# A gated linear recurrence with a causal convolution behind it: a new order of operations and transfers, and a shorter setup

## The chip, the cores and the metric

The kernel runs on one core of a Trainium2 chip. The metric is device time in microseconds (us) from start to end of one execution. The kernel before takes 310.14 us, the median of 3 runs (310.02 to 310.45). The profile is one execution of it, with a span of 309.0 us from the first to the last instruction.

The engines are named as the profile names them: PE (TensorE, matmuls), PEld (its weight loads), DVE (VectorE), ACT (ScalarE), POOL (GpSimd), SP (SyncE, which here only issues loads). ACT also issues the stores, from its own instruction queue.

## The reference

Inputs x, r_gate and i_gate are 4 x 6336 x 256 in float32 (25,344 tokens of 256 channels in all). In short:

```python
a_base = 1 / (1 + exp(-a_param))
a_t    = exp(8 * sigmoid(r_gate) * log(clip(a_base, 1e-6, 1 - 1e-6)))
xg     = sqrt(max(1 - a_t * a_t, 1e-6)) * sigmoid(i_gate) * x
h      = a_t[:, t] * h + xg[:, t]          # along the 6336 tokens of each batch; y[:, t] = h
gate   = sigmoid(causal convolution of y over 5 tokens, per channel)
out    = (gate * (y @ w_val)) @ w_out
```

## The kernel before

The tokens are cut into 27 chunks: 512, then 23 of 1024, then 512, 512 and 256. Each chunk passes through a row of operations. A text called PLAN lists all of them, one word for each (`exp.7.0.-1` is the exp of chunk 7, half 0 of the channels; the last number is a PSUM bank), and the kernel emits them in that order. Every engine executes its own operations in the order of PLAN.

| word | engine | what it does | us of one (1024 tokens, or 512 for conv, val, out, tg, gv, xg, copies) |
|---|---|---|---|
| ldri, ldx | SP | loads r and i, and x, 1 MB each | |
| tanh | ACT | tanh of half of r and i, in one instruction | 3.6 |
| srT | PE | transposes of r | |
| exp | ACT | a_t, for half of the channels | 1.2 |
| e | POOL | a_t squared | 1.9 |
| s1, u | POOL | (1 + tanh of i), and that times x | 1.9 and 4.1 |
| xc, ux | PE, DVE | for chunks 0 and 1 alone: x copied to PSUM, then u made on DVE | |
| sq | ACT | square root for up to three chunks; the table of functions is changed before and after | |
| nT, xg, xgT | PE, DVE, PE | transpose, product, transpose back | xg 0.7 |
| scan | DVE | the recurrence | 2.3 |
| conv, tg | PE, ACT | convolution, tanh of it | tg 1.0 |
| val, gv, out | PE, DVE, PE | y @ w_val, product with the gate, product with w_out | gv 1.2 |
| osbD or osbA | DVE or ACT | copy of the result from PSUM | 1.2 or 1.0 |
| store | ACT queue | 256 KB or less to out | |

The buffers (three chunks of gates, two of x, four of u) and the loads and stores:

```python
X_PE = [0, 1]      # the chunks whose u is made through PE and DVE
NRI = 3; NX = 2; NU = 4; NOSB = 5; NTG = 2; NGV = 2

with tc.manual_schedule():
    ...
    def op_ldri(k, bank):
        c = k[0]
        n = CHUNKS[c]
        for e, src in ((0, rf), (1, if_)):
            nc.sync.dma_start(gate[:, slot(c, e), 0:n * H].rearrange("p (j d) -> p j d", d=D), toks(src, c, 0, n))

    def op_ldx(k, bank):
        c = k[0]
        nc.sync.dma_start(xr[:, c % NX, 0:CHUNKS[c] // P, :], toks(xf, c, 0, CHUNKS[c]))
    ...
    def op_store(k, bank):
        c, s = k
        o, n = subs[c][s]
        nc.scalar.dma_start(toks(of, c, o, n), osb[:, nth[k] % NOSB, 0:n // P * D].rearrange("p (q d) -> p q d", d=D))
```

Each transfer counts up a semaphore when it has landed. The program has eight of these for all loads and stores together, and hands them out in turn, in the order in which the transfers are emitted: the ninth takes the semaphore of the first, and so waits until the first has landed before it is issued. The wait stands in the queue of the engine that issues the transfer.

The setup computes the constant of each channel, and the weights are cast on ACT:

```python
nc.scalar.preload_act_table_set("natural_log_exp_and_others")
...
nc.scalar.activation(out=kex[:], in_=kps, func=ACT.Exp, scale=-1.0)
nc.vector.tensor_scalar(out=ksig[:], in0=kex[:], scalar1=1.0, scalar2=None, op0=ALU.add)
nc.vector.reciprocal(out=ksig[:], in_=ksig[:])
nc.vector.tensor_scalar(out=ksig[:], in0=ksig[:], scalar1=1e-6, scalar2=1.0 - 1e-6, op0=ALU.max, op1=ALU.min)
nc.scalar.activation(out=kln[:], in_=ksig[:], func=ACT.Ln)
nc.scalar.preload_act_table_set("exp_and_others")
...
def op_wc(k, bank):
    for hk in range(H):
        nc.scalar.copy(out=wv[:, hk, :, :]..., in_=wvf[:, hk, :]...)
    nc.scalar.activation(out=wo2[:], in_=wof, func=ACT.Copy, scale=0.5)
...
def op_tanh(k, bank):
    c = k[0]
    w = CHUNKS[c] * H
    s0 = slot(c, 0)
    nc.scalar.activation(out=tgate[:, s0:s0 + 2, 0:w], in_=gate[:, s0:s0 + 2, 0:w], func=ACT.Tanh, scale=0.5)
...
def op_u(k, bank):
    c = k[0]
    if c in X_PE:
        return op_ux((c, CHUNKS[c] // 256 - 1), bank)
    u, t = gated(c)
    xt = xr[:, c % NX, 0:CHUNKS[c] // P, :].rearrange("p (w b) d -> p w b d", b=2)
    nc.gpsimd.tensor_tensor(out=u, in0=t, in1=xt, op=ALU.mult)
```

Of the kernel before, what the change touches and what calls it, by code (L numbers as in the profile page):

```python
# [8 lines left out]
P = 128  # L9
HP = 64  # L10
SUBN = 512
BANK = 512
CONV_K = 5
# [3 lines left out]
X_PE = [0, 1]  # L17
# [7 lines left out]
NTG = 2  # L25
NGV = 2
# [7 lines left out]
ldri.0.-1 ldri.1.-1 ldx.0.-1 ldx.1.-1 ldri.2.-1 ldw.-1 tanh.0.-1 srT.0.0.7 srT.0.1.5 exp.0.1.-1 exp.0.0.-1 e.0.0.-1  # L34
tanh.1.-1 e.0.1.-1 xc.0.1.0 xc.0.0.6 ux.0.0.-1 xc.1.2.1 u.0.-1 sq.0.1.-1 ux.1.2.-1 srT.1.0.0 ldri.3.-1 xc.1.1.5
ldx.2.-1 nT.0.0.7 srT.1.1.4 exp.1.0.-1 xg.0.0.-1 ux.1.1.-1 exp.1.1.-1 xc.1.0.0 tanh.2.-1 xc.1.3.5 e.1.1.-1 ux.1.0.-1
e.1.0.-1 wc.-1 srT.2.0.3 s1.2.-1 srT.2.1.2 xgT.0.0.4 exp.2.0.-1 scan.0.0.-1 exp.2.1.-1 e.2.0.-1 u.1.-1 tanh.3.-1
ldx.3.-1 ldri.4.-1 e.2.1.-1 u.2.-1 srT.3.1.3 srT.3.0.6 xgT.0.1.1 sq.1.2.-1 s1.3.-1 ldx.4.-1 ldri.5.-1 nT.2.0.7
nT.2.1.0 u.3.-1 xg.2.0.-1 exp.3.1.-1 xg.2.1.-1 nT.1.1.7 scan.0.1.-1 nT.1.0.5 tanh.4.-1 xg.1.1.-1 conv.0.0.0 xg.1.0.-1
xgT.2.0.3 e.3.1.-1 ldx.5.-1 xgT.1.1.4 ldri.6.-1 xgT.1.0.2 scan.1.1.-1 tg.0.0.-1 exp.3.0.-1 s1.4.-1 srT.4.1.1  # L40
exp.4.1.-1 scan.1.0.-1 val.0.0.4 e.3.0.-1 tanh.5.-1 srT.4.0.6 gv.0.0.-1 conv.1.0.0 u.4.-1 scan.2.0.-1 xgT.2.1.7
tg.1.0.-1 srT.5.1.5 srT.5.0.4 exp.4.0.-1 scan.2.1.-1 val.1.0.0 exp.5.1.-1 e.4.1.-1 ldx.6.-1 ldri.7.-1 exp.5.0.-1
gv.1.0.-1 conv.2.0.6 tanh.6.-1 e.5.1.-1 out.0.0.4 conv.1.1.0 osbD.0.0.-1 e.4.0.-1 val.2.0.2 tg.1.1.-1 val.1.1.4
e.5.0.-1 store.0.0.-1 tg.2.0.-1 out.1.0.0 conv.2.1.6 osbD.1.0.-1 s1.5.-1 sq.3.3.-1 gv.1.1.-1 u.5.-1 gv.2.0.-1
out.2.0.0 out.1.1.4 osbD.2.0.-1 osbD.1.1.-1 s1.6.-1 nT.3.1.3 ldri.8.-1 nT.3.0.2 ldx.7.-1 val.2.1.0 tg.2.1.-1 xg.3.0.-1
xg.3.1.-1 store.1.0.-1 u.6.-1 tanh.7.-1 gv.2.1.-1 xgT.3.1.7 nT.4.0.6 scan.3.1.-1 srT.6.0.1 srT.6.1.4 xgT.3.0.2
nT.4.1.0 nT.5.1.5 exp.6.0.-1 xg.4.0.-1 s1.7.-1 ldri.9.-1 xg.4.1.-1 exp.6.1.-1 srT.7.0.1 xg.5.1.-1 ldx.8.-1 nT.5.0.6
scan.3.0.-1 exp.7.0.-1 out.2.1.4 e.6.1.-1 tanh.8.-1 xgT.4.1.3 srT.7.1.7 xg.5.0.-1 conv.3.0.0 e.7.0.-1 osbD.2.1.-1
scan.4.1.-1 conv.3.1.4 u.7.-1 store.1.1.-1 tg.3.0.-1 xgT.4.0.6 srT.8.0.2 tg.3.1.-1 scan.4.0.-1 srT.8.1.0 exp.7.1.-1
val.3.1.4 exp.8.1.-1 gv.3.1.-1 e.6.0.-1 conv.4.1.6 ldx.9.-1 exp.8.0.-1 ldri.10.-1 xgT.5.0.3 store.2.0.-1 tg.4.1.-1  # L50
out.3.1.4 e.7.1.-1 scan.5.0.-1 tanh.9.-1 xgT.5.1.7 val.3.0.0 e.8.0.-1 conv.4.0.2 gv.3.0.-1 osbD.3.1.-1 e.8.1.-1
tg.4.0.-1 scan.5.1.-1 val.4.1.4 s1.8.-1 val.4.0.0 sq.6.3.-1 out.3.0.2 gv.4.1.-1 u.8.-1 gv.4.0.-1 osbD.3.0.-1 out.4.0.0
out.4.1.2 osbD.4.0.-1 srT.9.1.6 osbD.4.1.-1 nT.8.1.5 s1.9.-1 ldri.11.-1 nT.6.1.4 xg.8.1.-1 exp.9.1.-1 conv.5.0.2
ldx.10.-1 xg.6.1.-1 store.3.0.-1 tanh.10.-1 e.9.1.-1 nT.6.0.4 nT.7.1.1 xg.6.0.-1 nT.7.0.0 xgT.6.1.5 xg.7.0.-1 u.9.-1
xgT.6.0.4 xg.7.1.-1 srT.9.0.6 scan.6.0.-1 nT.8.0.7 exp.9.0.-1 conv.5.1.0 tg.5.0.-1 scan.6.1.-1 tg.5.1.-1 xgT.7.1.2
s1.10.-1 ldri.12.-1 store.2.1.-1 tanh.11.-1 val.5.1.0 ldx.11.-1 xg.8.0.-1 srT.10.1.3 srT.10.0.6 gv.5.1.-1 e.9.0.-1
val.5.0.4 conv.6.1.0 gv.5.0.-1 exp.10.1.-1 u.10.-1 srT.11.1.7 scan.7.1.-1 store.3.1.-1 store.4.1.-1 conv.6.0.4
tg.6.1.-1 exp.10.0.-1 srT.11.0.1 xgT.7.0.0 tg.6.0.-1 val.6.0.2 scan.7.0.-1 exp.11.0.-1 e.10.0.-1 out.5.0.4 ldri.13.-1
store.4.0.-1 ldx.12.-1 exp.11.1.-1 osbD.5.0.-1 out.5.1.0 e.10.1.-1 tanh.12.-1 conv.7.0.6 osbD.5.1.-1 e.11.0.-1
val.6.1.4 gv.6.0.-1 gv.6.1.-1 out.6.0.2 tg.7.0.-1 e.11.1.-1 store.5.1.-1 osbD.6.0.-1 xgT.8.1.6 xgT.8.0.7 s1.11.-1  # L60
out.6.1.4 scan.8.1.-1 sq.9.3.-1 val.7.0.2 u.11.-1 gv.7.0.-1 osbD.6.1.-1 conv.7.1.2 scan.8.0.-1 srT.12.0.1 srT.12.1.6
nT.9.0.0 nT.9.1.4 s1.12.-1 ldri.14.-1 nT.11.0.5 xg.9.0.-1 exp.12.0.-1 nT.10.0.7 ldx.13.-1 xg.9.1.-1 store.6.1.-1
xg.11.0.-1 store.5.0.-1 tg.7.1.-1 xgT.9.1.0 e.12.0.-1 scan.9.1.-1 exp.12.1.-1 out.7.0.2 tanh.13.-1 val.7.1.4 u.12.-1
osbD.7.0.-1 conv.8.0.0 gv.7.1.-1 nT.10.1.2 xgT.9.0.3 xg.10.1.-1 tg.8.0.-1 srT.13.0.6 scan.9.0.-1 s1.13.-1 ldri.15.-1
store.7.0.-1 tanh.14.-1 val.8.0.0 ldx.14.-1 out.7.1.4 xg.10.0.-1 e.12.1.-1 conv.8.1.2 gv.8.0.-1 srT.13.1.7 osbD.7.1.-1
store.6.0.-1 tg.8.1.-1 u.13.-1 xgT.10.0.1 srT.14.0.0 scan.10.0.-1 exp.13.0.-1 srT.14.1.4 out.8.0.2 exp.14.0.-1
xgT.10.1.6 store.7.1.-1 osbD.8.0.-1 exp.13.1.-1 conv.9.0.0 e.14.0.-1 exp.14.1.-1 scan.10.1.-1 ldx.15.-1 val.8.1.2
ldri.16.-1 tg.9.0.-1 nT.11.1.7 val.9.0.4 e.13.0.-1 store.8.0.-1 tanh.15.-1 gv.8.1.-1 conv.9.1.0 gv.9.0.-1 e.14.1.-1
out.8.1.2 val.9.1.4 osbD.8.1.-1 tg.9.1.-1 e.13.1.-1 xg.11.1.-1 store.8.1.-1 gv.9.1.-1 xgT.11.0.3 out.9.0.0 s1.14.-1
# [71 lines left out]
def kernel(  # L141
# [54 lines left out]
    with tc.manual_schedule():  # L196
# [16 lines left out]
        def slot(c, e):  # L213
            return 2 * (c % NRI) + e
# [292 lines left out]
```

## Time and profile before

| | value |
|---|---|
| time, median of 3 runs | 310.14 us |
| span of the profiled execution | 309.0 us |
| DVE busy | 252.3 us |
| POOL busy | 235.2 us |
| moved by DMA | 104.74 MB, 339 GB/s over the span |
| table loads on ACT between the chunks (L472) | 22, 28.2 us |

A busy time is the sum of an engine's instructions; what is missing to the span is idle time. A line such as "L290" is a line of the kernel. In the list of waits, "ACT gate L290 <- DMA x: 3.9, 1, 3.9" means that ACT, before an instruction of line 290, waited 3.9 us in total, once, at most 3.9 us, for what stands on the right. "SPq" and "ACTq" are the queues that issue transfers: SPq L220 and L224 issue the loads of gates and of x, ACTq L459 the stores. L304 is exp, L310 the square on POOL, L345 u, L354 the square root, L407 conv, L417 the gate's tanh.

The tail of the kernel is the stretch after the last exp, when all loads but the last have landed and the chunks still under way are finished.

### The profile page before, as it was taken

What the parts mean: (1) busy time and instruction counts of PE and PEld (TensorE: products, weight loads), DVE (VectorE), ACT (ScalarE), POOL (GpSimd) and SP (SyncE); (2) the same over time, 40 slices, a digit from 0 to 9 for tenths busy, and PEclk for the clock granted to TensorE, in tenths of its full rate; (3) what the DMA queues carried; (4) which work ended last, traced back from release to release, by engine and by line L of the source; (5) the groups of instructions that cost most, each with busy time, mean ns of one, the idle gap of its engine ahead of it and who ended that gap; (6) DMA issues with size and microseconds to landing.
All of it is one profiled execution on the core that took longest, in us unless ns stands there. A gap on an engine that the chain in (4) does not pass through costs nothing.

```text
span 309.0 us, 6335 instructions
## 1 busy us (share of the span) xinstructions
PE 248.1 (80%) x2627; PEld 167.7 (54%) x2627; DVE 252.3 (82%) x208; ACT 278.5 (90%) x185; POOL 235.2 (76%) x118
## 2 busy tenths in 40 slices
PE   0582577958888898799489998988899987999994
PEld 0232454447546564557257665675666655565763
DVE  1052079479898989999499999999999998989893
ACT  6799999999999999998699999999999979868632
POOL 3229998997998999899996799989959993038000
PEclk9995589999999999999979999999999999999999
DMA  7999999998997999999999997999897764182555
GB/s 288 427 360 422 382 417 364 365 352 318 389 377 263 413 414 422 421 421 421 428 423 365 363 390 280 376 426 424 336 369 309 285 249 137 69 337 109 200 212 237
DMA packets 19466, 104.74 MB, mean 339 GB/s; under 512 B 2151, under 2 KB 2670, under 8 KB 10606
## 3 DMA queue, kind: packets, MB, share of 16 engines
q1 hardware_dynamic: 12224, 78.39, 65.0%
q10 hardware_dynamic: 7214, 25.96, 21.0%
q8 instruction: 20, 0.33, 0.4%
q14 instruction: 8, 0.07, 0.1%
HBM read 78.39 MB, written 25.95 MB: 338 GB/s over the span
## 4 chain that ended last, share of the span: by engine, by line
PE 24%; DMA 21%; POOL 18%; ACT 17%; issue 11%; DVE 6%; ACTq 1%; SPq 1%; POOLq 0%; DVEq 0%
DMA gate<-in_i_gate_dram 13%; POOL uring L345 10%; PE pp L407 7%; PE pp L439 6%; DMA xr<-in_x_dram 6%; ACT gate L290 5%; POOL ering L310 5%; ACT tgr L417 4%; PE pp L425 4%; ACT aring L304 4%; POOL gate L318 3%; PE pp L367 3%; DMA out_dram<-osb 3%; DVE yring L395 3%; PE pp L327 2%
## 5 line engine op out<-in xcount | busy, mean ns | idle before, releaser
L310 POOL TENSOR_TENSOR ering<-aring 128x1024 f32<-128x1024 f32 (+2 forms) x54 | 93.6, 1754 | 36.7 <-ACT aring L304 35.1
L395 DVE TENSOR_TENSOR_SCAN yring<-aring,yring,pp 128x1024 bf16<-128x1024 f32 (+2 forms) x52 | 113.4, 2193 | 4.1 <-PE pp L382 4.1
L345 POOL TENSOR_TENSOR uring<-gate,xr 128x2048 bf16<-128x2048 bf16 (+2 forms) x25 | 96.0, 3845 | 4.3 <-PE pp L382 2.6
L290 ACT ACTIVATE gate<-gate 128x4096 bf16<-128x4096 f32 (+2 forms) x27 | 90.2, 3340 | 7.6 <-DMA xr<-in_x_dram 3.9
L407 PE MATMUL pp<-yring,diag 64*64 64x512 bf16 (+13 forms) x1224 | 65.3, 341 | 5.2 <-DVE yring L395 2.2
L430 DVE SCALAR_TENSOR_TENSOR gvr<-tgr,pp 128x1024 bf16<-128x1024 bf16 (+1 forms) x50 | 59.4, 1200 | 8.9 <-ACT tgr L417 6.7
L439 PE MATMUL pp<-wo,gvr 128*128 128x256 bf16 x396 | 52.7, 279 | 13.9 <-DVE gvr L430 7.9
L304 ACT ACTIVATE aring<-pp,khf 128x1024 f32<-128x1024 bf16 (+2 forms) x54 | 59.3, 1144 | 3.9 <-PE pp L295 2.2
L417 ACT ACTIVATE tgr<-pp 128x1024 bf16<-128x1024 f32 (+1 forms) x50 | 50.5, 1024 | 10.0 <-PE pp L407 8.6
L439 PEld LDWEIGHTS <-gvr 128*128 128x128 bf16 x396 | 42.5, 115 | 23.8 <-DVE gvr L430 11.1
L425 PE MATMUL pp<-yring,wv 128*128 128x512 bf16 (+1 forms) x200 | 50.5, 377 | 6.1 <-DVE osb L454 2.2
L454 DVE COPY osb<-pp 128x1024 f32<-128x1024 f32 x41 | 49.0, 1211 | 6.1 <-PE pp L439 5.9
L318 POOL TENSOR_SCALAR gate<-gate 128x2048 bf16<-128x2048 bf16 (+2 forms) x25 | 44.5, 1781 | 5.4 <-ACT gate L290 5.4
L407 PEld LDWEIGHTS <-diag 64*64 64x64 bf16 x1224 | 30.6, 107 | 30.6 <-issue 14.5
L354 ACT ACTIVATE ering<-ering,b 128x4096 bf16<-128x4096 f32 (+4 forms) x16 | 46.4, 2932 | 0.1
L374 DVE TENSOR_TENSOR uring<-uring,pp 128x1024 bf16<-128x1024 bf16 (+1 forms) x50 | 32.0, 672 | 12.7 <-PE pp L367 12.5
L295 PE MATMUL pp<-ident_b,gate 128*128 128x128 bf16 x396 | 31.4, 229 | 13.2 <-ACT gate L290 11.1
L295 PEld LDWEIGHTS <-gate 128*128 128x128 bf16 x396 | 26.6, 103 | 21.9 <-ACT gate L290 14.0
L367 PE MATMUL pp<-ident_f,ering 128*128 128x128 f32 x198 | 32.3, 303 | 5.4 <-ACT ering L354 3.9
L382 PE MATMUL pp<-ident_f,uring 128*128 128x128 f32 x198 | 31.5, 282 | 6.1 <-ACT tgr L417 2.8
L367 PEld LDWEIGHTS pp<-ident_f,ering 128*128 128x128 f32 x198 | 27.8, 208 | 11.6 <-ACT ering L354 4.8
L425 PEld LDWEIGHTS <-wv 128*128 128x128 bf16 x200 | 18.8, 98 | 23.9 <-issue 11.1
(33 smaller groups left out, 86.9 us busy)
## 6 DMA issues: line engine op xcount, KB each, us to landing
out_dram<-osb ACTq DMA_DIRECT2D x49, 512.0 KB, 7.9
gate<-in_r_gate_dram SPq DMA_DIRECT2D x23, 1024.0 KB, 11.7
gate<-in_i_gate_dram SPq DMA_DIRECT2D x23, 1024.0 KB, 9.6
xr<-in_x_dram SPq DMA_DIRECT2D x23, 1024.0 KB, 10.0
gate<-in_r_gate_dram SPq DMA_DIRECT2D x3, 512.0 KB, 7.7
gate<-in_i_gate_dram SPq DMA_DIRECT2D x3, 512.0 KB, 10.7
xr<-in_x_dram SPq DMA_DIRECT2D x3, 512.0 KB, 3.4
yring<-in_moe_w_val_dram SPq DMA_DIRECT2D x1, 256.0 KB
```

The costliest lines, as they stand in the source:

```text
L290: nc.scalar.activation(out=tgate[:, s0:s0 + 2, 0:w], in_=gate[:, s0:s0 + 2, 0:w], func=ACT.Tanh, scale=0.5)
L295: nc.tensor.transpose(out=ppb[:, bank * 2 * BANK + j * P:bank * 2 * BANK + (j + 1) * P], in_=tgate[:, slot(c, 0), j * D + h * P:j * D + (h ...
L304: nc.scalar.activation(out=dst, in_=src, func=ACT.Exp, scale=khf[:, h:h + 1], bias=khf[:, h:h + 1])
L310: nc.gpsimd.tensor_tensor(out=ering[:, c % NE, h * n:(h + 1) * n], in0=a, in1=a, op=ALU.mult)
L345: nc.gpsimd.tensor_tensor(out=u, in0=t, in1=xt, op=ALU.mult)
L367: nc.tensor.transpose(out=pp[:, d0:d0 + P], in_=src[:, w, :], identity=ident_f[:])
L395: nc.vector.tensor_tensor_scan(out=yring[:, h, y0:y0 + n], data0=aring[:, c % NA, h, 0:n], data1=src, initial=prev, op0=ALU.mult, op1=ALU.add)
L407: nc.tensor.matmul(out=pp[col * HP:(col + 1) * HP, b0 + d0:b0 + d1], lhsT=diag[r * HP:(r + 1) * HP, h, kk, :], rhs=yring[r * HP:(r + 1) * ...
L417: nc.scalar.activation(out=tgr[:, nth[k] % NTG, :, 0:n], in_=two(live["conv", k], n), func=ACT.Tanh, scale=0.5)
L425: nc.tensor.matmul(out=pp[:, (bank + m) * BANK:(bank + m) * BANK + n], lhsT=wv[:, hk, m, :], rhs=yring[:, hk, y0:y0 + n], start=(hk == 0), ...
L430: nc.vector.scalar_tensor_tensor(out=gvr[:, nth[k] % NGV, :, 0:n], in0=tgr[:, nth[k] % NTG, :, 0:n], scalar=1.0, in1=two(live["val", k], n ...
L439: nc.tensor.matmul(out=pp[:, bank * BANK + j * D:bank * BANK + (j + 1) * D], lhsT=gvr[:, nth[k] % NGV, m, 0:n].rearrange("c (p q) -> c q p ...
```

## The change

PLAN is replaced as a whole. The order of all operations is another one, found by a search that takes into account that the transfers use eight semaphores in turn; the loads of r and i have words of their own (ldr, ldi) and stand apart in it. Each transfer gets an ordering edge to the one before, so that the order in which they take the semaphores is the plan's. The edges are of a kind that carries no wait on the chip (NoSync). The search moved five output copies more to ACT: PLAN has 14 osbA and 36 osbD for 9 and 41. The groups of square roots are the same.

The rest of the diff:

- u of chunks 0 and 1 is made on POOL as for all other chunks; xc and ux are gone.
- tanh of chunk 0 is split into one for r and one for i.
- The log of the sigmoid is computed as -ln(1 + exp(-a)) in one activation, and clipped afterwards; the sum, the reciprocal and the clip ahead of the Ln are gone from DVE.
- The weights are cast on POOL, not ACT.
- The gated value overwrites the gate's tanh (three buffers, where there were two for each).
- Small setup tiles lie in an output buffer that is not yet used.
- POOL is left out of the hand-made schedule; its instructions keep the program's order by a mark of their own.

```diff
-X_PE = [0, 1]
+X_PE = []
-NTG = 2
-NGV = 2
+NTG = 3
 ...
-ldri.0.-1 ldri.1.-1 ldx.0.-1 ldx.1.-1 ldri.2.-1 ldw.-1 tanh.0.-1 srT.0.0.7 srT.0.1.5 exp.0.1.-1 exp.0.0.-1 e.0.0.-1
-tanh.1.-1 e.0.1.-1 xc.0.1.0 xc.0.0.6 ux.0.0.-1 xc.1.2.1 u.0.-1 sq.0.1.-1 ux.1.2.-1 srT.1.0.0 ldri.3.-1 xc.1.1.5
+ldr.0.-1 ldi.0.-1 ldi.1.-1 ldr.1.-1 ldx.0.-1 ldw.-1 ldi.2.-1 tanh.0.-1 srT.0.0.3 ldr.2.-1 tanhi.0.-1 srT.0.1.1
+exp.0.1.-1 exp.0.0.-1 e.0.1.-1 ldx.1.-1 e.0.0.-1 s1.0.-1 sq.0.1.-1 nT.0.0.7 u.0.-1 tanh.1.-1 wc.-1 xg.0.0.-1 ldi.3.-1
 ... (the rest of PLAN)
-    with tc.manual_schedule():
+    with tc.manual_schedule(engines={mybir.EngineType.SP, mybir.EngineType.Activation, mybir.EngineType.DVE,
+                                     mybir.EngineType.PE}):
 ...
+        keep = tc.keep_in_program_order
+        turn = []
+
+        def dma(queue, dst, src):
+            i = queue.dma_start(dst, src)
+            if turn:
+                tc.add_manual_dep(i.ins, turn[-1].ins.name,
+                                  mybir.DependencyInfo(mybir.DependencyClass.NoSync, mybir.DependencyReason.DATA),
+                                  reason="turn of the transfers")
+            turn.append(i)
 ...
-        nc.vector.tensor_scalar(out=ksig[:], in0=kex[:], scalar1=1.0, scalar2=None, op0=ALU.add)
-        nc.vector.reciprocal(out=ksig[:], in_=ksig[:])
-        nc.vector.tensor_scalar(out=ksig[:], in0=ksig[:], scalar1=1e-6, scalar2=1.0 - 1e-6,
-                                op0=ALU.max, op1=ALU.min)
-        nc.scalar.activation(out=kln[:], in_=ksig[:], func=ACT.Ln)
+        nc.scalar.activation(out=kln[:], in_=kex[:], func=ACT.Ln, bias=1.0)
 ...
-                nc.scalar.copy(out=wv[:, hk, :, :]..., in_=wvf[:, hk, :]...)
-            nc.scalar.activation(out=wo2[:], in_=wof, func=ACT.Copy, scale=0.5)
+                keep(nc.gpsimd.tensor_scalar(out=wv[:, hk, :, :]..., in0=wvf[:, hk, :]...,
+                                             scalar1=1.0, scalar2=1.0, op0=ALU.mult, op1=ALU.mult))
+            keep(nc.gpsimd.tensor_scalar(out=wo2[:], in0=wof, scalar1=0.5, scalar2=1.0, op0=ALU.mult, op1=ALU.mult))
 ...
-            nc.scalar.activation(out=tgate[:, s0:s0 + 2, 0:w], in_=gate[:, s0:s0 + 2, 0:w], func=ACT.Tanh, scale=0.5)
+            s0, s1 = slot(c, 0), slot(c, 0) + (1 if c == 0 else 2)
+            nc.scalar.activation(out=tgate[:, s0:s1, 0:w], in_=gate[:, s0:s1, 0:w], func=ACT.Tanh, scale=0.5)
+
+        def op_tanhi(k, bank):
+            ...
+            nc.scalar.activation(out=tgate[:, slot(c, 1), 0:w], in_=gate[:, slot(c, 1), 0:w], func=ACT.Tanh, scale=0.5)
```

## The prediction

> **What bounds the kernel now.** I read the page's table of busy times first, then busy time by stage, then the list of waits, then the order of time around the longest waits. The page:
>
> ```profile
> PE 248.1 (80%) x2627; PEld 167.7 (54%) x2627; DVE 252.3 (82%) x208; ACT 278.5 (90%) x185; POOL 235.2 (76%) x118
> ```
>
> ACT (ScalarE) is fullest: 278.5 of 309.0 us, so 30.5 us idle. The stages say where. Columns of the busy-time-by-stage view: stretch, its length, busy us of PE, PE weight load, DVE, ACT, POOL, then PE clock, DMA share, GB/s. I cut at 274.4 us, where the last exp (chunk 26) starts.
>
> ```profile
> 8.00:21.00 13.00, 9.75 (x39) 4.86 (x37) 3.57 (x6) 11.07 (x8) 2.04 (x2) 1.00 1.05 398
> 21.00:60.00 39.00, 25.19 (x231) 16.64 (x232) 18.62 (x15) 37.89 (x25) 37.38 (x17) 0.78 0.98 390
> 60.00:120.00 60.00, 48.32 (x549) 33.83 (x548) 54.75 (x44) 59.45 (x35) 57.05 (x26) 1.00 0.95 365
> 120.00:180.00 60.00, 50.68 (x536) 34.92 (x537) 54.64 (x43) 55.98 (x35) 53.84 (x25) 0.97 1.01 404
> 180.00:240.00 60.00, 53.44 (x579) 37.00 (x578) 59.50 (x47) 59.80 (x36) 55.17 (x26) 1.00 0.93 366
> 258.00:274.40 16.40, 14.12 (x166) 9.46 (x166) 14.58 (x12) 13.85 (x14) 0.00 (x0) 1.00 0.46 171
> 274.40:309.00 34.60, 29.79 (x348) 19.12 (x346) 28.50 (x25) 19.29 (x21) 10.19 (x9) 0.98 0.53 209
> ```
>
> Between 60 and 120 us and between 180 and 240 us ACT is busy 59.45 and 59.80 of 60: nothing can be gained there but by taking work off ACT. After 274.4 us ACT is busy 19.29 of 34.60 and PE 29.79: the tail is PE's, with DVE (28.50) close. Before 274.4 us ACT is busy 278.45 - 19.29 = 259.2 us, hence idle 15.2. These 15.2 us and the 34.6 us tail are what the change can work on.
>
> What ended ACT's waits:
>
> ```profile
> ACT tgr L417 <- PE pp L407: 8.6, 7, 3.6
> ACT gate L290 <- DMA xr<-in_x_dram: 3.9, 1, 3.9
> ACT gate L290 <- DMA gate<-in_i_gate_dram: 3.6, 4, 1.6
> ```
>
> The second is odd: the gate tanh (L290) doesn't read x. The order of time shows it:
>
> ```profile
> 144.80 1.07 ACT L417 ACTIVATE tgr<-pp 128x1024 bf16<-128x1024 f32 x1
> 149.31 0.34 ACTq L459 DMA_DIRECT2D out_dram<-osb  x1
> 149.78 3.62 ACT L290 ACTIVATE gate<-gate 128x4096 bf16<-128x4096 f32 x1 [3.90 <-DMA xr<-in_x_dram]
> ```
>
> A store stands in ACT's queue ahead of the tanh and is issued only at 149.31. Counted in program order, its semaphore was last taken, eight transfers earlier, by a load of x issued at 136.43. ACT stood still behind a store that had to wait for a stranger. The transfer queue of SP shows the same in sum:
>
> ```profile
> SPq L220 <- POOL uring L345: 88.7, 12, 13.7
> SPq L224 <- POOL uring L345: 73.0, 9, 18.4
> SPq L224 <- DMA xr<-in_x_dram: 17.5, 5, 6.0
> SPq L220 <- DMA gate<-in_r_gate_dram: 7.4, 2, 7.2
> ```
>
> SP waits mostly for POOL's product u (162 us: buffers to come free), but some 25 us here for other transfers.
>
> **What the Trainium skill says.** "DMA: Bandwidth & Descriptors", "Anatomy of one DMA": the wait for a semaphore is made on the issuing sequencer, before dispatch. The 3.90 us above agree. "Issuing engines are not separate DMA queues" (same page): loads and stores share the same 16 engines. The trace agrees: a 1 MB load takes 9.6 to 11.7 us to land at the median (page, part 6), while the last store, 256 KB alone, takes 2.1 us. So the order of transfers decides who gets the bandwidth. "ScalarE: Activation LUTs", "What ACT_TABLE_LOAD costs": about 1283 ns, plus a drain of 1380 ns. Here the 22 loads of L472 average 1283 ns, but the next op starts 0.02 us after one (59.91 + 1.28, then 61.21): I charge 1.28 us. "SBUF — State Buffer", "SBUF: two separate sides", says DVE and POOL can lock each other out of a shared port, for DVE ops with two SBUF inputs among others; DVE's large ops here take one input from PSUM, and u on POOL ranges only to 4147 ns with a median of 4117. I charge no lock-out for work moved to POOL.
>
> **The change, part by part.**
>
> *ACT's work.* Five more output copies go to ACT (osbA 9 to 14, osbD 41 to 36): 5 x 1.01 = +5.0 us. The weight casts leave it: 2 x 0.39 + 0.63, -1.3 us on the path after overlap. The first tanh is split: two of 1024 columns at 1.05 (as for chunk 26) for one of 1.91, +0.2. Square roots keep their groups, so table loads stay as many. ACT: 278.5 + 5.0 - 1.3 + 0.2 = 282.4 us. The bound itself thus gets longer by 3.9.
>
> *Other engines.* DVE loses 5 x 1.21 and six ux at 0.72: -10.4, to about 242 (a few tenths more from the short setup). POOL gains u of chunks 0 and 1 (2.16 + 4.12), their s1 (1.05 + 1.90) and the weight casts, which I estimate at 1.3 from s1 (1.90 us for 2048 columns, here 1024 in three ops): +10.5, to 245.7. All of it falls before about 45 us. PE loses 8.8 us of x copies (L327), at the start.
>
> *Start.* Idle of ACT there that should go: the tanh of r can run as soon as r has landed, and the Ln needs no trip over DVE (first gate tanh at 5.75, with waits of 0.64 and 0.54 before it): 0.5. The second half of the split tanh covers the 1.13 us in which exp waits for PE's transposes. Tanh of chunk 1 now comes after sqrt, so its 0.48 wait goes; the 0.60 behind the x copies goes too. Against that, exp of chunk 1 follows its tanh directly and waits about 0.7 for transposes. Net: 0.5 + 1.1 + 0.5 + 0.6 - 0.7 = 2.0.
>
> *Order of transfers.* The 3.9 us at 149 us, and 0.45 behind a store at 114.28, should go: 4.35. The new order was searched with the semaphores in view, so the search could see these. The 162 us of SP waiting for u are no saving: two x buffers and three gate buffers stay as they are. I allow 1.0 us for waits of the same kind in new places. The ordering edges order without a wait, so they cost nothing. Gated values overwriting the tanh tile (three buffers for two plus two) change no duration.
>
> Idle before the last exp: 15.2 - 2.0 - 4.35 + 1.0 = 9.85 us.
>
> *Tail.* By the two plans, behind the last exp stand 8 conv, 9 val, 10 out and 8 transposes of u before, and 7, 8, 9 and 7 after: one each less, 1.2 + 0.9 + 1.0 + 0.4 = 3.5 us of PE. DVE has one long scan (2.34), one gv and two copies less (about 6). PE's tail was 34.6; it becomes about 31.1. ACT has one copy more there: 20.3 us of its work, well inside.
>
> *Sum.* ACT before the last exp 282.4 - 20.3 = 262.1; plus idle 9.85 = 272.0; plus tail 31.1 = 303.1 us of span. The timed runs exceed the profiled span by 1.1 (310.14 against 309.0), which gives 304.2, rounded to 304.
>
> **Rivals.** *POOL becomes the bound.* It is busy 57.05 of 60 us already. For the square root of chunks 9 to 11 (begun at 121.6) I count 98.1 us of POOL work up to the last square it needs, starting at 10.3: 108.4, slack 13. After: 108.6 from about 8, so 116.6, against ACT ready around 122: slack 5. It should fit, but a late u delays the next loads. If POOL runs out, ACT waits and the time is 308 to 311. *The transfers become the bound.* DMA share is 0.93 to 1.01 from 8 to 240 us, but with rates from 365 to 404 GB/s for stretches and 428 in the best slice; 104.7 MB at 420 would need 249 us. If buffer release, not order, decides when loads start, only part of the 4.35 us comes back and new waits for loads appear: 306 to 309. *The tail is not PE's work but its chain.* ACT waits 8.6 us for conv (L407) there; a chain of sqrt, transpose, scan, conv, tanh, product and out behind the late chunks could keep the 34.6 us: 307 to 308. *More comes off.* If the search removed also the waits of 240 to 274 us, where POOL stands idle 16.4 us while loads of the last chunks arrive late, idle falls to 5: 299.
>
> **Range and chances.** The sum has the plus of ACT work certain (3.9), the start fairly sure (2.0), transfers (3.35 net) and tail (3.5) less so. All fail: 310 + 2. All come and the late waits go too: 299. I take 298.5 to 310. Two per cent faster means below 303.9, about my centre: 0.50. Within 2%: 0.42. Slower: 0.08.
>
> **What would show it.** Right: ACT busy near 282; no ACT wait put down to a transfer over 1 us in mid-kernel; first gate tanh near 5.2; ACT idle before the last exp near 10; that exp near 272; 31 us after it. Wrong if: POOL's waits vanish and ACT waits for squares (sqrt L354 with idle time before it), tanh waits for gate loads in the middle, or the tail is as long as before.

## The result and the profile after

The changed kernel takes 323.54 us (median of 4 runs, 323.15 to 325.85); the kernel before took 310.19 us beside it. The ratio is 1.0445, with a 95% interval of 1.0396 to 1.0494: slower by 4.4%, where 2% faster was predicted.

The table of busy times of the changed kernel, as the prediction showed it of the kernel before:

```profile
PE 251.5 (78%) x2615; PEld 169.7 (53%) x2615; DVE 242.9 (75%) x195; ACT 283.1 (88%) x188; POOL 245.2 (76%) x125
```

The work is what the prediction counted: ACT 283.1 us, DVE 242.9, POOL 245.2. But the span is 321.9 us, so ACT now stands idle for 38.8 us, where it was 30.5. The busy time by stage says where (stretch, length, busy us of PE, PEld, DVE, ACT, POOL, PE clock, DMA share, GB/s); the last exp starts at 288.80:

```profile
21.00:60.00 39.00, 25.79 (x243) 17.76 (x239) 19.26 (x15) 38.68 (x22) 39.00 (x17) 0.78 0.94 383
60.00:120.00 60.00, 47.94 (x521) 32.98 (x520) 48.29 (x38) 51.98 (x33) 53.09 (x25) 0.94 0.91 337
120.00:180.00 60.00, 49.40 (x491) 32.58 (x485) 51.48 (x41) 57.41 (x33) 49.69 (x23) 0.97 0.96 378
180.00:240.00 60.00, 50.18 (x536) 33.47 (x535) 53.87 (x43) 54.64 (x33) 55.09 (x26) 0.97 0.92 358
240.00:288.80 48.80, 44.94 (x480) 30.36 (x476) 42.61 (x33) 42.13 (x37) 28.41 (x16) 0.93 0.59 223
288.80:321.90 33.10, 27.19 (x332) 17.93 (x328) 23.53 (x22) 20.23 (x21) 6.17 (x7) 0.96 0.51 204
```

Up to 60 us ACT is nearly full, 38.68 of 39. Then it loses in the very stretches that were full: 51.98 of 60 where it was 59.45, and 54.64 where it was 59.80. From 120 to 180 us, where the stop of 3.9 us stood before, it gains: 57.41 for 55.98. Between 60 and 120 us the transfers slow down too, 337 GB/s in place of 365. After the last exp little has changed: 33.1 us against 34.6 before.

ACT's waits (us in total, times, longest):

```profile
ACT tgr L436 <- PE pp L426: 11.5, 12, 2.3
ACT gate L304 <- DMA gate<-in_i_gate_dram: 8.9, 6, 2.2
ACT tgr L436 <- DMA out_dram<-osb: 2.9, 1, 2.9
ACT gate L304 <- POOL uring L364: 2.8, 1, 2.8
```

Line 304 is the gate tanh. It waits 8.9 us for loads of i, where it was 3.6. So look at who issues them. The waits of SP's queue:

```profile
SPq L221 <- POOL uring L364: 107.1, 21, 13.3
SPq L221 <- DMA out_dram<-osb: 66.5, 14, 12.6
SPq L221 <- PE pp L314: 55.2, 13, 14.3
```

The second line is new. SP only issues loads, and no load needs a store; yet it waits 66.5 us, in 14 places, for stores to land. The kernel before has no such line, but for the wait at its end. (In this view a wait counts from the end of the instruction before, so time in which the load's own buffer was not yet free is in it.) What that does is best seen in order of time. First SP's queue, then ACT's:

```profile
97.20 0.33 SPq L221 DMA_DIRECT2D gate<-in_i_gate_dram  x1
106.23 0.33 SPq L221 DMA_DIRECT2D gate<-in_r_gate_dram  x1
106.61 0.42 SPq L221 DMA_DIRECT2D xr<-in_x_dram  x1
107.12 0.38 SPq L221 DMA_DIRECT2D gate<-in_i_gate_dram  x1
```

```profile
98.44 3.62 ACT L304 ACTIVATE gate<-gate 128x4096 bf16<-128x4096 f32 x1
...
106.09 3.62 ACT L304 ACTIVATE gate<-gate 128x4096 bf16<-128x4096 f32 x1 [2.19 <-DMA gate<-in_i_gate_dram]
...
119.83 3.62 ACT L304 ACTIVATE gate<-gate 128x4096 bf16<-128x4096 f32 x1 [2.82 <-POOL uring L364]
```

SP issues i of chunk 11 at 97.20 and then nothing for 9 us. Next in its queue is r of chunk 12, issued at 106.23. Counted in program order, its semaphore was held eight transfers earlier by the store of chunk 3, half 1. That store stood in ACT's queue until 97.46 and landed at 106.15, 0.07 us before the load was issued. r.12's own buffer had been free since 86.1 us. Behind r.12 stand x.10, whose buffer was free from 97.2, and i.12, whose buffer u of chunk 9 freed at 105.06. So the store cost i.12 itself only 2 us of waiting; but the three loads then went out within 0.9 us of each other, and i.12 took 12.5 us to land, at 119.67. (In e4 below, r.12 and x.10 go out 7 us ahead of i.12, and it lands in 9.4.) Tanh of chunk 12 began at 119.83. Its wait is put down to a u, but the event just before it, by 0.16 us, is i.12's landing. The Trainium skill says in "DMA: Bandwidth & Descriptors", "Anatomy of one DMA — SWDGE (gpsimd) path", that DMA engines do not wait on semaphores and any such wait is made on the issuing sequencer, before dispatch. The trace of SP's queue agrees: 9 us without an issue, with r.12's buffer free.

In this trace eight loads are issued within 0.1 us after the landing of the store that held their semaphore: x.5 (47.69), r.9 (68.65), x.9 (90.12), r.12, x.11 (120.15), x.12 (121.33), x.13 (139.82) and x.15 (160.27). With i.14 (136.59, 0.46 us after its store) they were held for 43 us in all, worked out load by load from the time at which buffer and queue were free to the store's landing; x.11 alone for 12.6 us. The count of loads that follow a store on their semaphore is not what grew: 21, against 22 before. But before, such a store had landed 2 to 19 us ahead of the load. The searched order put young stores in front of loads.

### The profile page after: what moved, and what is told of

It is laid out like the page before. It is cut to its first block, busy times and chain, and to the rows that moved or that the text cites. A ratio compares the mean times of both kernels' runs of the same rounds, so it can differ in the third digit from the quotient of the medians.

```text
span 321.9 us, 6322 instructions
## 1 busy us (share of the span) xinstructions
PE 251.5 (78%) x2615; PEld 169.7 (53%) x2615; DVE 242.9 (75%) x195; ACT 283.1 (88%) x188; POOL 245.2 (76%) x125
## 3 DMA queue, kind: packets, MB, share of 16 engines
q10 hardware_dynamic: 7214, 25.96, 20.2%
## 4 chain that ended last, share of the span: by engine, by line
DMA 27%; PE 27%; ACT 15%; DVE 12%; POOL 10%; issue 7%; ACTq 1%; SPq 0%; DVEq 0%; POOLq 0%
DMA out_dram<-osb 10%; PE pp L426 8%; DMA xr<-in_x_dram 7%; DMA gate<-in_i_gate_dram 7%; PE pp L458 6%; DVE yring L414 6%; POOL uring L364 6%; ACT gate L304 6%; PE pp L444 4%; ACT ering L373 3%; PE pp L314 3%; PE pp L386 3%; DVE tgr L449 3%; DMA gate<-in_r_gate_dram 3%; POOL ering L329 2%
## 5 line engine op out<-in xcount | busy, mean ns | idle before, releaser
L364 POOL TENSOR_TENSOR uring<-gate,xr 128x2048 bf16<-128x2048 bf16 (+2 forms) x27 | 102.1, 3785 | 15.7 <-DMA xr<-in_x_dram 9.4
L449 DVE SCALAR_TENSOR_TENSOR tgr<-tgr,pp 128x1024 bf16<-128x1024 bf16 (+1 forms) x50 | 59.4, 1200 | 21.4 <-PE pp L444 16.4
L426 PE MATMUL pp<-yring,diag 64*64 64x512 bf16 (+12 forms) x1224 | 68.4, 357 | 4.4 <-DVE yring L414 2.7
L458 PE MATMUL pp<-wo,tgr 128*128 128x256 bf16 x396 | 53.9, 285 | 11.2 <-DVE tgr L449 6.7
L444 PE MATMUL pp<-yring,wv 128*128 128x512 bf16 (+1 forms) x200 | 52.9, 390 | 9.5 <-ACT tgr L436 6.4
L458 PEld LDWEIGHTS <-tgr 128*128 128x128 bf16 x396 | 43.1, 117 | 22.8 <-DVE tgr L449 12.4
L473 DVE COPY osb<-pp 128x1024 f32<-128x1024 f32 (+1 forms) x36 | 42.8, 1200 | 14.1 <-PE pp L458 9.4
L337 POOL TENSOR_SCALAR gate<-gate 128x2048 bf16<-128x2048 bf16 (+2 forms) x27 | 47.4, 1756 | 7.5 <-ACT gate L304 7.5
L314 PE MATMUL pp<-ident_b,gate 128*128 128x128 bf16 x396 | 33.7, 238 | 19.9 <-ACT gate L304 13.9
L314 PEld LDWEIGHTS <-gate 128*128 128x128 bf16 x396 | 28.3, 107 | 28.3 <-ACT gate L304 19.0
L386 PE MATMUL pp<-ident_f,ering 128*128 128x128 f32 x198 | 33.1, 308 | 12.5 <-ACT ering L373 10.2
## 6 DMA issues: line engine op xcount, KB each, us to landing
xr<-in_x_dram SPq DMA_DIRECT2D x23, 1024.0 KB, 10.8
```

The costliest lines, as they stand in the source:

```text
L314: nc.tensor.transpose(out=ppb[:, bank * 2 * BANK + j * P:bank * 2 * BANK + (j + 1) * P], in_=tgate[:, slot(c, 0), j * D + h * P:j * D + (h ...
L364: keep(nc.gpsimd.tensor_tensor(out=u, in0=t, in1=xt, op=ALU.mult))
L386: nc.tensor.transpose(out=pp[:, d0:d0 + P], in_=src[:, w, :], identity=ident_f[:])
L426: nc.tensor.matmul(out=pp[col * HP:(col + 1) * HP, b0 + d0:b0 + d1], lhsT=diag[r * HP:(r + 1) * HP, h, kk, :], rhs=yring[r * HP:(r + 1) * ...
L444: nc.tensor.matmul(out=pp[:, (bank + m) * BANK:(bank + m) * BANK + n], lhsT=wv[:, hk, m, :], rhs=yring[:, hk, y0:y0 + n], start=(hk == 0), ...
L449: nc.vector.scalar_tensor_tensor(out=tgr[:, nth[k] % NTG, :, 0:n], in0=tgr[:, nth[k] % NTG, :, 0:n], scalar=1.0, in1=two(live["val", k], n ...
```

## The experiments

Theory T: the order of transfers costs the time. Rivals: P, GpSimd's 10.5 us of new early work delays every later u and so the loads; H, loads held in the queue behind others whose buffers are not free; and later U, the new order of computing leaves too little time between u of one chunk, which frees a buffer, and the tanh that needs the next load in it. "Old plan" means the order of operations and transfers of the kernel before, in the code of the changed kernel. Each ratio is to the kernel before on the same chip, with its 95% interval. The times in us are medians of all executions; the ratios leave out those in a slower state (7 of 20 of e1, 1 of 4 of e3, which is the one profiled, 2 of 12 of e10, 1 of 18 of e12, 4 of 18 of e15, 3 of 20 of e16).

### The old plan in the new code: e1 and e1b

```diff
-PLAN of the change, X_PE = []
+PLAN of before (ldri split in two, first tanh split), X_PE = [0, 1]
-NTG = 3
+NTG = 4      # e1b only
```

e1 keeps three buffers, so in four of fifty parts a tg overwrites a gated value still to be read; e1b has none of that.

> The changed kernel with the plan of before (r and i loads side by side, u of chunks 0 and 1 through PE and DVE): all of the rest of the change (short setup, split first tanh, weights cast on POOL, gated value over the gate's tanh, ordering edges) without its order. If the loss lies in the order of the plan, by whatever path: 306 to 310 us. If the rest of the change costs (the shared three buffers of tanh and gated value, or the edges): over 314.

> The old plan, as in the first run, with four shared buffers for tg and gv where the changed kernel has three: the old plan needs four, or a tg overwrites a buffer that an out has still to read (so in the first run, in parts 5, 8, 9 and 43). Everything else is the changed kernel's: split gate loads, split first tanh, short setup, edges that hold the order of transfers. Theory P (the plan, not the rest, costs the time): 307 to 311 us. If three buffers held the first run back: 303 to 306. If the edges or the split loads cost time by themselves: above 312.

e1: 309.49 us, ratio 0.9947 (0.9922 to 0.9971). e1b: 307.66 us, 0.9915 (0.9894 to 0.9937). So the split loads, the ordering edges, the short setup and (with four of them) the merged buffers are no cost: together they gain 0.9%. What makes the change slow is in the new plan.

### The new plan with other transfers: e2, e3, e4

```diff
 (e2)  the computing of the new plan; loads and stores in the sequence of before
 (e3)  the new plan; loads in its order, stores in their places, but interleaved
       so that 2 loads follow a store on their semaphore (21 in the change)
 (e4)  the same, interleaved so that 34 do; each load as early as it may stand
-... xg.6.0 store.3.1 ldr.11 ldx.8 ldr.10 ldi.10 ldx.9 u.8 ... scan.7.0 store.4.0 ldr.12
+... store.3.0 ldr.11 ldx.8 ldr.10 u.7 ldi.10 ... store.3.1 ldx.9 u.8 ldi.11 ldr.12   # e4
```

> The changed kernel with its order of compute kept, and the transfers in the sequence of before, each as soon as that sequence and its buffer allow, stores two ACT instructions behind their copy. Theory T (the order of transfers lost the time, loads waiting behind stores): 304 to 312 us. Theory C (the order of compute or the 10 us more on POOL lost it): 318 to 324.

> The changed kernel; order of the loads on SP, places of the stores on ACT and all compute kept. Only the merging of loads and stores into one sequence differs, so that 2 loads take a semaphore that a store had before, for 21. Theory T in its narrow form (a load waits for the semaphore of a late store): 306 to 313 us, and hardly any SP wait for a store. Theory H (loads in a wrong order on SP, one with no free buffer ahead of one that has it): 318 to 323. Theory C: 320 to 324.

> As the run before, but merged so that 34 loads take a semaphore that a store had before, for 21. Narrow theory T: 328 to 345 us. Theories H and C: 320 to 325.

e2: 343.03 us, 1.1048 (1.0992 to 1.1103), slower than either theory had it. The old sequence of transfers doesn't fit the new order of computing: SP waits 188.7 us for u there. e3: 316.0 us, 1.0168 (1.0124 to 1.0211). e4: 314.65 us, 1.0141 (1.0087 to 1.0196). Theory T in its narrow form, the number of pairings, falls: 2 and 34 of them give the same time (for 34 it had 328 to 345 us). But both runs, one with hardly a load behind a store and one with many loads behind mostly older stores, are faster than the change by 7.5 and 8.9 us. SP's queue in e4:

```profile
SPq L221 <- DMA out_dram<-osb: 17.5, 6, 7.4
```

```profile
94.95 0.33 SPq L221 DMA_DIRECT2D gate<-in_i_gate_dram  x1
95.38 0.37 SPq L221 DMA_DIRECT2D gate<-in_r_gate_dram  x1
95.84 0.38 SPq L221 DMA_DIRECT2D xr<-in_x_dram  x1
```

SP waits 17.5 us for stores, not 66.5 (in e3 not at all), and r.12, issued at 106.23 in the change, goes out at 95.38. In all three kernels every engine executes the same operations in the same order, loads and stores included; only the semaphores fall to the transfers differently. So **which transfer a load takes its semaphore from, and so how young the store there is, is worth some 8 of the 13.4 us.** The rest, 4.5 us over the kernel before and 7 over e1b, is another matter. The first line of e4's page:

```profile
PE 244.4 (78%) x2588; PEld 167.4 (54%) x2615; DVE 243.2 (78%) x195; ACT 282.4 (90%) x188; POOL 245.5 (79%) x125
```

Of e4's span of 312.5 us ACT is idle for 30.1, as before the change (30.5). Against the kernel before, e4 loses the 3.9 us of ACT's work that the new plan adds, and has next to none of the saving of idle time that the prediction promised.

### GpSimd's early work: e5, e6, e6b

```diff
 (e5)  new plan as e3, but
-X_PE = []          s1.0 u.0 s1.1 u.1 on GpSimd
+X_PE = [0, 1]      xc, ux on TensorE and VectorE
 (e6)  old plan as e1b, but
-X_PE = [0, 1]
+X_PE = []          ... wc s1.2 e.2.0 s1.1 u.1 e.2.1
 (e6b) the same, but
+                   ... s1.1 u.1 e.1.1 e.1.0 wc s1.2 e.2.0
```

> The new plan with its transfers merged as in the third run (e3, 316.0 us), but the first two x chunks go the old way again: TensorE copies them, VectorE gates them, and s1 of chunks 0 and 1 is gone. GpSimd loses some 9 us of work before 26 us. Theory P: 305 to 311 us, the u of chunk 2 starts 5 us or more earlier than at the new plan, and so do the loads behind it. Theory H: 313 to 318, since the loads wait in the queue behind others as before.

> The same old plan with four buffers, but the first two x chunks are not copied by TensorE and gated by VectorE: GpSimd does s1 and u of chunks 0 and 1, as in the new plan. Theory P (GpSimd's early burden of about 10.5 us, of s1 1.0 and 1.9, u 2.1 and 4.1, is what delays every later u, and with it the loads of i and x): 314 to 320 us, and the waits of u and tanh grow in the first 60 us. Theory H (the order and place of the loads, not GpSimd's early work): 307 to 311, within 1% of the run with the copies.

> The run with s1 and u of chunks 0 and 1 on GpSimd in the old plan (314.8 us) put u of chunk 1 behind e of chunk 2, where it ended at 35.1 us, and x.3, which waits for its buffer, was issued at 35.1 in place of 21.8. Here s1 and u of chunk 1 stand directly before e of chunk 1, where GpSimd was idle for 6.3 us; nothing else differs. If only the late x.3 cost the time: 305 to 309 us, x.3 issued by 23 us. Theory P (any such work on GpSimd costs it): 311 to 315.

e5: 319.21 us, 1.0319 (1.0264 to 1.0374), slower than e3 and than either theory had it, and no run shows why. e6: 314.78 us, 1.0139 (1.0108 to 1.0170). e6b: 306.4 us, 0.9894 (0.9864 to 0.9923). Theory P, which e6 by itself would bear out, falls: the same GpSimd work that costs 7 us in e6 costs nothing in e6b. What e6 had wrong was one place in a queue: u of chunk 1 ended at 35.1 us, and x.3, which waits for its buffer, was issued at 35.14 in place of 21.84. Thirteen microseconds on one load at the start became 7 at the end. In e6b x.3 is issued at 20.51. e6b is the fastest kernel here with the right output, 1.1% ahead of the one before. The first line of its page, and its stages:

```profile
PE 239.9 (79%) x2615; PEld 165.0 (54%) x2615; DVE 247.4 (81%) x200; ACT 277.1 (91%) x183; POOL 245.4 (81%) x125
60.00:120.00 60.00, 48.34 (x550) 34.36 (x543) 54.67 (x44) 59.88 (x36) 57.02 (x27) 1.00 0.94 367
120.00:180.00 60.00, 52.23 (x585) 36.07 (x583) 58.15 (x46) 59.07 (x36) 57.39 (x26) 1.00 1.01 423
180.00:240.00 60.00, 53.84 (x590) 37.51 (x589) 59.50 (x47) 59.56 (x37) 55.16 (x25) 1.00 0.91 356
```

ACT is busy 59.88, 59.07 and 59.56 of 60 us: it hardly waits there.

### The order of the loads: e7 to e11

```diff
 (e7)  old plan as e1b; no load follows a store on its semaphore (22 did)
 (e8)  new plan as e4, loads in the order in which their buffers came free in e4
-i.8 r.9 i.9 x.7 r.11 x.8 r.10 i.10 x.9 i.11 r.12
+r.9 x.7 i.8 r.10 x.8 i.9 r.11 r.12 x.9 i.10
 (e9)  old plan as e1b, each r of chunks 5 to 23 behind the x that follows it
-r.13 i.13 x.12 r.14 i.14 x.13
+i.13 x.12 r.13 i.14 x.13 r.14
 (e10) old plan as e1b, loads in the order in which their buffers came free in e1b
 (e11) new plan as e4, only late r loads moved ahead
-i.11 r.12 x.10 i.12 x.11 i.13 x.12 r.13 r.15 r.14 i.14
+r.12 i.10 x.9 i.11 x.10 i.12 x.11 r.13 r.14 i.13 x.12 r.15 i.14
```

> The old plan with four buffers, with the loads in their old order and the stores in their old places, but interleaved so that no load takes a semaphore that a store held last (22 loads do in the old order of the transfers). If a load behind a store costs time only where the store is recent (in the kernel before the stores had landed 2 to 19 us before): within 1% of the run without this, 306 to 311 us. If pairing costs time as such: 301 to 305.

> The new plan as in the run with most pairings (e4, 314.7 us): the same compute order, the same places of the stores; only the order of the loads in SyncE's queue is changed, to the order in which their buffers came free in that run's trace. There r.13 stood behind i.13 and x.12, was issued at 118.2 us although its buffer was free at 108.1, landed at 131.3 and held ScalarE for 2.5 us. Theory H (a load that stands in the queue behind loads whose buffers are not free costs the time): 306 to 311 us, the waits of ScalarE for gate loads gone or under 3 us in all. Theory P (GpSimd's early work, or the new order of the computing): 313 to 317.

> The old plan with four buffers (307.7 us), where each r load of chunks 5 to 23 is moved behind the x load that follows it, much as the new plan has it (r.13 behind i.13 and x.12); the computing and the places of the stores are the same. Theory H: 312 to 320 us, with new waits of tanh for r loads. If the old plan's order of computing has so much slack that the place of the r loads does not matter: 306 to 310, and H alone does not explain the new plan.

> The old plan with four buffers, loads in the order in which their buffers came free in its own trace (so r.7, r.14, r.16 and r.17 would be issued some 5 to 9 us earlier). Theory H in full: 303 to 306 us. If its tanh waits for no r load that matters: 306.5 to 309, as without the change.

> The new plan of e4 (314.7 us) with only those r loads moved ahead in SyncE's queue whose buffers had come free more than 2 us before that of a load ahead of them: r.12, r.13, r.14, r.17, r.19, r.25, by one to three places (i stays ahead of x, which e8 turned round). Theory H (loads held in the queue by others): 307 to 312 us. Theory U (in the new order of computing, u of chunk c-3, which frees the i buffer, ends too shortly before tanh of chunk c for a transfer to fit in: 9.4 us on the mean in e4, 13.5 in the old plan, and a transfer takes 7 to 13): 313 to 316, since the i loads still come no earlier.

| run | us | ratio | interval |
|---|---|---|---|
| e7 | 309.59 | 0.9991 | 0.9976 to 1.0007 |
| e8 | 329.07 | 1.0615 | 1.0581 to 1.0649 |
| e9 | 359.75 | 1.1629 | 1.1579 to 1.1679 |
| e10 | 309.87 | 0.9989 | 0.9964 to 1.0013 |
| e11 | 314.5 | 1.0136 | 1.0096 to 1.0176 |

Theory H as I put it falls. e9 shows how dear a bad place is: 52 us over e1b for r loads standing behind one x load, far more than the 312 to 320 us of H. But putting loads in the order of readiness (e8, e10) makes both plans slower, e8 by 14 us, e10 by 2. In e8 hardly a load is held in the queue any more (from 60 us on, the most between buffer free and issue is 3.7 us; e4 has up to 14.8). But I had put x ahead of i where one u frees both, and r.9 ahead of i.8: i.8 is issued at 69.96 behind r.9 and x.7, lands at 80.30, and tanh of chunk 8 starts at 80.45, 7 us later than in e4. Here order by need counts for more than order by readiness. e11, which keeps i ahead of x and moves only the late r loads, ends at e4's time: H explains none of the remainder. A trace line of e4 that had led me to H,

```profile
131.37 3.62 ACT L304 ACTIVATE gate<-gate 128x4096 bf16<-128x4096 f32 x1 [2.48 <-DMA gate<-in_r_gate_dram]
```

was a wait whose removal (0.2 us of waits for r loads are left in e11) changed the time by nothing that can be told from noise.

### From u to tanh: e12 to e16

The distance from the end of u of chunk c-3 (which frees the i buffer) to the start of tanh of chunk c, and the time tanh starts after its later gate has landed, both worked out from the traces for the 19 chunks 5 to 23:

| kernel | u to tanh, mean us | gates landed before tanh, mean us | tanh within 0.5 us of the landing |
|---|---|---|---|
| before | 14.3 | 4.1 | 2 of 19 |
| e6b (old plan) | 13.5 | 3.5 | 2 |
| after | 10.0 | 0.9 | 11 |
| e4 (new plan) | 9.4 | 1.0 | 10 |
| e14 | 10.6 | 1.9 | 8 |

A 1 MB load of i takes 10.1 us at the median to land in e6b and 8.4 in e4 (page, part 6). With 13.5 us there are 3.4 to spare, with 9.4 there is one: much what the second column shows. That is Theory U. The mean alone doesn't give the time, though: e14, with 10.6, is 16 us slower than e4. Its runs:

```diff
 (e12) new plan as e4;   (e13) old plan as e6b
-ldx.4 ... ldx.26         # both; u gates an old x, the output is another
 (e14) old plan as e6b, u of 12 chunks later by one or two e on GpSimd
-u.10 ... e.10.0 ... e.10.1
+e.10.0 ... e.10.1 u.10
 (e15) new plan as e4, u of 10 chunks earlier by one or two e
 (e16) e12 with five output copies of chunks 17, 18, 22 back on VectorE
-osbA.17.1 osbA.18.0 osbA.18.1 osbA.22.1 osbA.22.0
+osbD.17.1 osbD.18.0 osbD.18.1 osbD.22.1 osbD.22.0
```

> The new plan of e4 with the loads of x left out from chunk 4 on (u then gates an old x, so the output is another; the computing is the same): three quarters of the load bytes are left, and u waits for no x. Theory U, and any in which the new order only loses by its transfers: 297 to 305 us, ScalarE's waits for gate loads gone. If the new order of computing is slow by itself (more work of ScalarE, or its order of PE and VectorE): 309 or more.

> The old plan with four buffers and GpSimd's u placed early (e6b, 306.4 us), with the loads of x left out from chunk 4 on in the same way. Theory U: it had time for its transfers already, so only 0 to 4 us less, 302 to 306, and the new plan without x is as fast or faster. If the x loads' share of the bandwidth costs all plans alike: 295 to 300.

> The old plan of e6b (306.4 us), where u of 12 of the chunks from 6 to 22 is moved behind the next one or two e (1.9 us each) on GpSimd, so that u ends up to 3.8 us later and so do the i and x loads behind it; the loads' order is the same. Theory U: 310 to 320 us, with tanh within half a microsecond of the landing of its gates in many chunks, as in the new plan. If the distance from u to tanh does not matter: 305 to 308.

> The new plan of e4 (314.7 us) with u of ten chunks (4, 6, 7, 9, 10, 13, 16, 18, 21, 23) moved ahead of the one or two e that stand before it on GpSimd, so up to 3.8 us earlier; the order of the loads is the same, each at its earliest place. It is the reverse of e14. Theory U: 308 to 312 us. If u then only waits for its x load, whose buffer comes free no earlier: 313 to 320, with more waits of u for x than the 6.4 us of e4.

> The run of the new plan without the x loads (e12, 308.5 us), with five of the fourteen output copies on ScalarE (of chunks 17, 18 and 22) back on VectorE; the old plan has nine on ScalarE. If the 5.6 us between e12 and e13 are ScalarE's five copies (1.01 us each): 302.5 to 305 us. If it is the new order itself: 307 to 310.

| run | us | ratio | interval |
|---|---|---|---|
| e12 | 308.53 | 0.9941 | 0.9917 to 0.9965 |
| e13 | 302.96 | 0.9758 | 0.9727 to 0.9790 |
| e14 | 330.92 | 1.0653 | 1.0608 to 1.0699 |
| e15 | 312.81 | 1.0057 | 1.0032 to 1.0082 |
| e16 | 311.52 | 1.0021 | 0.9999 to 1.0044 |

e14 is the strong one: 1.9 or 3.8 us on twelve u cost 24.5 us, more than Theory U had. (Loads and stores are interleaved anew there, but no load from chunk 4 on is held by a semaphore.) ACT's waits of e6b, then of e14:

```profile
ACT gate L304 <- DMA gate<-in_i_gate_dram: 4.4, 4, 1.8
```

```profile
ACT gate L304 <- DMA gate<-in_i_gate_dram: 23.5, 9, 6.4
```

So the distance matters, in the plan that had it. The reverse gives back less: e15 gains 1.8 us on e4, 0.8% by the ratios, just short of what Theory U expected. Part of this can be the interleaving, which is new here too: no load of e15 is held by a semaphore, where e4's were for 20 us in all. GpSimd's u waits 10.8 us for x loads there (6.4 in e4): part of what u gains in place it loses again at x.

Without the x loads the new plan still takes 5.6 us more than the old. Theory U had expected it at 297 to 305 us and no slower than e13, so U can't be the whole of the remainder. The transfers are hardly in the way any more: ACT's wait for i in e12 is

```profile
ACT gate L302 <- DMA gate<-in_i_gate_dram: 1.9, 2, 1.5
```

The busy times of e12, e13 and e16 show what is left:

```profile
PE 246.7 (80%) x2615; PEld 168.3 (55%) x2615; DVE 242.4 (79%) x195; ACT 282.6 (92%) x188; POOL 245.3 (80%) x125
```

```profile
PE 238.9 (79%) x2615; PEld 164.9 (55%) x2615; DVE 247.2 (82%) x200; ACT 277.0 (92%) x183; POOL 245.5 (82%) x125
```

```profile
PE 244.3 (79%) x2588; PEld 167.4 (54%) x2615; DVE 247.9 (80%) x200; ACT 278.4 (90%) x183; POOL 245.2 (79%) x125
```

ACT is idle 25.1 us in e12 (307.7 - 282.6) and 24.1 in e13 (301.1 - 277.0): they differ by ACT's work, five copies. It is tempting to stop there. e16 takes the five copies off ACT, and ACT's idle time grows to 30.5 us (308.9 - 278.4) and the run by 3 us, slower than either expectation. In this order the copies can't simply be moved back. So the five copies alone don't explain the 5.6 us; what does stays open.

One rival is untested: the clock that TensorE is granted. It was 0.998 to 0.999 in e13's executions and 0.98 to 1.00 in e6b's, but 0.937 to 0.975 in e12's, 0.951 to 0.969 in e4's and 0.937 to 0.953 in those of the changed kernel. PE is busy 246.7 us in e12 and 238.9 in e13, for nearly the same work. In e4 the clock is low where ACT stands still (0.85 from 120 to 140 us, ACT busy 15.78 of 20). No run changes the clock and keeps the order, so it isn't shown whether the low clock is a cause of lost time or follows from it.

### The account

| what | runs | us |
|---|---|---|
| the new code with the old plan | e1b against before | -2.3 |
| x's first chunks on GpSimd, u early | e6b against e1b (the intervals overlap) | -1.3 |
| the rest of the new plan: order of computing and of loads, five more copies on ACT, three buffers for four; 5.6 without x loads too (e12 against e13) | e4 against e6b | +8.3 |
| young stores ahead of loads on their semaphore | after against e4 | +8.9 |
| sum | | +13.6 |
| measured | after against before | +13.4 |

These are differences of medians taken at different times and on more than one chip, so each is good to about 1 us; by the ratios the last two steps are 2.5% and 3.0%. The steps lead from one kernel to the next, so the sum is no test of them. In the profiled spans the 8.3 (there 312.5 - 303.8 = 8.7) are 5.3 us of ACT's work and 3.4 of its idle time, and the 8.9 (321.9 - 312.5 = 9.4) are 0.7 of work and 8.7 of idle time. That the semaphores cost 7.5 to 8.9 is shown by e3 and e4. Of the 8.3 it is shown that they aren't GpSimd's early work (e5, e6b) nor the late r loads (e11); how they divide among the distance from u to tanh, the copies, the rest of the order and the clock is not shown.

## Why the prediction was wrong, step by step

- **ACT's work** (282.4 us): 283.1. Right, and so were VectorE and GpSimd.
- **Start** (2.0 us less idle): the first gate tanh begins at 4.31, not 5.2, and tanh of chunks 3, 5, 7 and 9 comes 2.0, 3.0, 2.9 and 4.0 us earlier than before. Right as a size. But the lead doesn't reach the end: tanh of chunk 10 comes at 98.4, against 99.1 before, of chunk 11, after a wait of 2.19 us for its i load, at 106.1 against 105.5, and of chunk 12 at 119.8 against 115.8.
- **Order of transfers** (4.35 us back, 1.0 of new waits, 9.85 us idle before the last exp): this is the step that failed. The last exp starts at 288.8 us, and of ACT's work 283.1 - 20.2 = 262.9 us lie before it, so 25.9 us are idle. The 3.9 us at 149 us did go: in e1b, with the old plan, tanh of chunk 15 starts 3.3 us earlier than before, after starts that agree within 0.4 us up to chunk 14. But where 1.0 us stood for "waits of the same kind in new places", some 17 came (25.9 less the 15.2 - 2.0 - 4.35 that should have stayed). Half of them are of that kind: e4, with the same order on every engine and other semaphores, has its last exp at 279.4 us and 17.3 us idle before it. I had taken a search "with the semaphores in view" as a search that avoids them; it had got rid of stores that waited for loads (eight before, none after) and put loads behind young stores, 43 us of holding in SP's queue, where every load behind a held one waits too. The profile's like is not gone either: one tg stands behind a store that waited for a store.

```profile
250.54 0.34 ACTq L221 DMA_DIRECT2D out_dram<-osb  x1
250.92 1.02 ACT L436 ACTIVATE tgr<-pp 128x1024 bf16<-128x1024 f32 x1 [2.87 <-DMA out_dram<-osb]
```

- **Not in the sum at all**: what the new plan costs apart from the semaphores, the other half of the 17 us. How it divides is not shown; the distance from u to tanh is the part of it that could be seen beforehand. I wrote that 162 us of SP waiting for u "are no saving" since the buffers stay as they are. But the total of that wait (107.1 us after, 142.9 in e4) says nothing of the time that is left for a load once u has ended, and this fell from 14.3 to 10.0 us. The question was in the two plans, word by word: u of chunk 10 stands ahead of both e of chunk 10 in the old, behind e.11.1 and e.10.1 in the new.
- **Tail** (31.1 us after the last exp): 33.1. The direction was right, the size too large by 2; TensorE's work there fell by 2.6 us, from 29.79 to 27.19, but the tail by 1.5 only, so TensorE's idle time in it grew. That is in part the rival "not PE's work but its chain".
- **Rivals.** "POOL becomes the bound" was wrong: it is full up to 60 us (39.00 of 39), but from 60 to 120 us it is busy 53.09 us where it was 57.05, and ACT waits only 0.2 us for its squares. "The transfers become the bound" foresaw that "new waits for loads appear", and the sign "tanh waits for gate loads in the middle" came true (8.9 us, line 304); but it gave them 306 to 309 us and set buffer release against order as alternatives. Order, by way of the semaphores, cost 8.9 us; what release has of the other 8.3 isn't separated. "More comes off" did not come: of 48.8 us from 240 to the last exp ACT is busy 42.13. The top of the range, 310, was the kernel before, below even the 312 of its own worst case: on the side of slower the sum had only ACT's 3.9 us and the 1.0 us of waits, although the change replaced the whole order.
- **Readings.** The 1.1 us from span to time compared two executions: the profiled one took 311.12 us, 2.1 more than its span (1.8 after), so the sum should have ended at 305.2. The load of x that held the store at 149.31 did have its semaphore, but stands six transfers ahead of it in PLAN, not eight: in the trace before, only 66 of 128 transfers share a semaphore with the one eight places ahead, and with the ordering edges of the change all 128 do. The DMA share from 8 to 240 us was 0.93 to 1.05.

## What to carry to other kernels

Where transfers take semaphores in turn, look at each load for the transfer that held its semaphore last and ask when that one lands, not how many such pairs there are: nine loads behind young stores cost some 8 us here, and 34 pairs with mostly older stores no more than 2 pairs. Before an order of operations is changed, take from the trace, chunk by chunk, the distance from the operation that frees a buffer to the one that needs the next load in it, and compare it with the time a load takes to land: at 13.5 us against 10.1 (e6b) ACT ran full, at 9.4 against 8.4 (e4) it didn't, though not for that reason alone. Split a difference into the work and the idle time of the fullest engine: e4's loss against the kernel before is all work. A wait seen once in a trace (r.13 in e4) is no measure of what its removal brings; the run is.

## What was not expected

- One load that is 13 us late in the first 40 us (x.3 in e6) cost 7 us at the end, and moving r loads back by a few places in one queue (e9) cost 52 us, on a core whose DMA rate over the span was 325 GB/s in the changed kernel and up to 423 in a 60 us stage of e6b.
- Rebuilding the interleaving so that no load follows a store (e7) made the old plan slower by 1.9 us (ratios 0.9991 and 0.9915, the intervals apart): in e1b the stores had landed 3 us or more before such loads, and of the new pairs one costs 2.5 us: a store issued at 199.36 waits for another to land, with a tg behind it in ACT's queue.
- The loads of x are a third of what is loaded, yet leaving nearly all of them out gains the old plan only 3.4 us (e13 against e6b): their transfer was almost wholly hidden there.
